# Pooled attention into a four-expert attention layer: score tiles of two heads and of 512 columns, split VectorE steps, a last batch in two parts, and a written-out order

## The chip, the cores and the metric

The kernel runs on one core of one Trainium2 chip. The metric is the device time of one execution in microseconds (us). The kernel before takes 198.42 us, the median of three runs (197.89, 198.42 and 199.59).

A core has five engines with instruction queues of their own: TensorE (PE) multiplies matrices, VectorE (DVE) and ScalarE (ACT) work element by element, GpSimd (POOL) does so too, and SyncE (SP) issues DMA transfers. Arithmetic results of PE go to PSUM, a small memory that DVE and ACT read; all other tiles lie in SBUF.

## The reference

The inputs are q, k and v (8 batches, 8 heads, 576 rows of 64), and the weights of four experts. Two attentions follow one another.

```python
# first attention: keys and values are means over 8 rows, so 72 of them
k_p = k.reshape(B, H, Sp, pool, D).mean(axis=3)
v_p = v.reshape(B, H, Sp, pool, D).mean(axis=3)
attn = softmax(q @ k_p.T / sqrt(64))
x = (attn @ v_p) as (8, 576, 512)

# second: a gate picks two of four experts for each row
logits = x @ w_gate
w = softmax over the two largest logits of a row, 0 for the others
for e in range(4):
    q, k, v = x @ wq[e], x @ wk[e], x @ wv[e]          # 576 x 64 each
    a = softmax(causal(q @ k.T / sqrt(64)))            # 576 x 576, lower triangle
    out += w[:, e] * (a @ v @ wo[e])                   # 576 x 512
```

The output is f32, 8 x 576 x 512. Every expert is computed for all rows, and the gate's weight is multiplied in at the normalisation.

## The kernel before, in words

**Tiles.** A row index of 576 is cut into five chunks: four of 128 and one of 64. Heads come in two halves of four; experts in two pairs (0, 1) and (2, 3), a pair filling 128 partitions with its two 64-wide projections. All matmul operands are bf16. Scores are computed transposed, keys on the partitions, so that exponentials can be used as the next product's operand as they are. A column of ones beside the values gives the softmax sum, and no maximum is subtracted. At the end a check looks at all reciprocals of the sums; if one lies outside a range, a branch runs a slow general version of all batches.

**Steps.** The program is planned as some hundred steps a batch, each named by two letters. For a batch:

- `ld`/`ln`: POOL issues the DMA loads of k, q and v in two halves each (line 324); the transfer turns f32 into bf16. `ln` marks the landing. The first batch's loads, the mask for the pooling product and the identity are issued in `first` (from line 780).
- `pk`, `pv`: the mean over 8 rows as a PE product with a mask `pm` (line 375); `kp`, `kz`, `kt`, `kT`: pooled keys copied, doubled, transposed on PE, copied. `vp`: pooled values copied.
- `qm`, `qc`: q transposed on PE and copied; for batches 5 to 7 by DMA instead (`qd` on SP, `ql` the landing).
- `am`, `ae`: pooled scores of one head on PE (line 437), and their exponential on ACT (line 462), for eight heads; and a ninth group with the one row in nine that a head's pairing leaves over (lines 450 and 472). `al`: POOL places the ninth group's results in the tile `eta` (line 483).
- `om`, `on`: output of the first attention for a chunk and half of the heads (line 493), then on DVE the reciprocal of the sum (505) and the product with it (506), into `xtm`.
- `xm`, `xc`: x transposed on PE and copied (batches 0 to 2), or `xd`, `xl`: turned by DMA (batches 3 to 7), into `xT`.
- `jm`, `jc`: the q and k projections of an expert pair and half of the rows, eight groups of four matmuls over 288 columns (line 550), and their copies. `vm`, `vc`: values of all experts and the gate's logits for a chunk (line 531), and the copies (541, 542).
- `ga`, `gs`, `ge`, `gb`, `gc`: the gate: maxima and selection on DVE (570 to 576), subtraction on POOL, exponential on ACT, weights on POOL, reciprocal and product on DVE.
- `bm`, `be`, `bk`: expert scores of a pair, in four parts of 400 columns for each of two experts (line 625), exponential on ACT (635), causal mask on POOL for each diagonal block (644).
- `bo`, `bn`: output of one expert for all five chunks, 15 matmuls (line 659); on DVE reciprocal (671), product with the gate's weight (673) and normalisation (674) into `osc`.
- `ot`, `oc`: `osc` transposed on PE and copied, or `od`, `ol`: turned by DMA (batches 2 to 6).
- `ym`, `yc`, `ys`: the product with wo for a chunk (line 695), the copy to SBUF (707), the store, issued on SP (712).
- At the end, `fl`, `fm`, `fc`: the range check on DVE, its sum on PE, the flag. The flag is then loaded into registers of all five engines (line 1319) and all five take the branch (1320).

**Turns.** A DMA transpose is issued on SP (line 778). All turns wait until the last input of the last batch has landed.

**Room.** Two PSUM tiles of two banks each, `jt`, serve the pooling products and both kinds of scores. Four one-bank PSUM tiles serve everything else. Inputs have three buffers for each of k, q and v; most work tiles have two, by the batch's parity.

**Order.** All instructions are emitted in one order, which sets the order in every engine's queue. It is found while the program is built, by the list scheduler `run_order` (line 169): it keeps a model time for each engine, takes the ready step with the lowest key (tables `RANK` and `EXTRA`, and the batch number times `SPAN`), and charges the durations of `COST`. Pooling products and both kinds of scores, and the dummy products between them, use 64 rows of the PE array, two matmuls side by side; all other products use 72 or 128 rows. The scheduler charges `TURN` for a change between the two kinds and prefers to stay in one. Where PE has nothing to do in the first 40 us of model time, it issues dummy products, four matmuls each (`filler`, line 745). Where a copy can go to ACT or DVE, the scheduler decides.

## Time and profile before

| | |
|---|---|
| profiled execution, device time | 198.56 us |
| its span, first to last instruction | 196.7 us |
| mean granted PE clock | 0.973 |
| input and weight bytes read from HBM | 30.42 MB |
| bytes written | 9.44 MB |
| loads of k, q, v, issue to landing (POOL's queue) | 10.2 to 10.3 us median |
| turns of x by DMA, issue to landing (SP's queue) | 2.5 us median |

The profile is of one execution. Its page lists each engine's busy time and share of the span, a picture of the span in 40 slices of 4.9 us (a digit is a tenth of the slice; the row PEclk is the clock that PE was granted, in tenths of full speed), the chain of work that ended last, followed back from the last instruction, and the costliest groups of instructions. PE overlaps its matmuls and its weight loads (PEld), and the ends of matmuls are modelled, so a busy share of PE is not PE at its best. The chain is a share of the span: what lies on it delays the end if it takes longer, and what does not may grow until it does.

### The profile page before, as it was taken

Reading aid. Unit: us, or ns where it says so; the run is one execution under the profiler, and the core shown is the slowest. Engines: PE = TensorE matmul, PEld = TensorE weight load, DVE = VectorE, ACT = ScalarE, POOL = GpSimd, SP = SyncE. Lnnn points to the kernel's source line nnn. Section 1 sums busy time; section 2 is a strip of 40 time slices with the busy share of each in tenths; the row PEclk is TensorE's granted clock in tenths of the full one; section 3 lists DMA queues with packets and bytes.
Section 4 is the critical chain, followed back from the end, with each engine's and each line's share of the span. In section 5 each row is a group of like instructions: output and inputs, shape, how many; then the busy total and the mean of one; then the engine's idle time right before and its main releaser. Section 6 shows DMA issues by size and latency. Waiting matters only on the chain.

```text
span 196.7 us, 6292 instructions
## 1 busy us (share of the span) xinstructions
PE 176.6 (90%) x2470; PEld 131.0 (67%) x2478; DVE 137.5 (70%) x478; ACT 139.7 (71%) x280; POOL 91.8 (47%) x197
## 2 busy tenths in 40 slices
PE   7999789899999899999789999889979999997740
PEld 7998668677889666766567658664657767575410
DVE  5122678938988787886934798769977868765840
ACT  3057588589994887866928896858979697788640
POOL 7957585765589553440405327314233533444100
PEclk9999999999999999999958999999999999999996
DMA  4999999999999999997955359362841559381561
GB/s 62 184 188 207 205 206 200 205 207 207 206 207 207 206 236 279 164 173 250 141 107 99 53 137 252 63 83 78 226 91 24 112 90 289 83 215 37 216 246 28
DMA packets 47666, 31.78 MB, mean 162 GB/s; under 512 B 28944, under 2 KB 43024, under 8 KB 47632
## 3 DMA queue, kind: packets, MB, share of 16 engines
q0 software_dynamic: 15056, 15.21, 47.3%
q1 hardware_dynamic: 32576, 16.13, 35.7%
q8 instruction: 20, 0.33, 0.7%
q14 instruction: 14, 0.11, 0.2%
HBM read 30.42 MB, written 9.44 MB: 203 GB/s over the span
## 4 chain that ended last, share of the span: by engine, by line
PE 65%; DMA 12%; DVE 9%; POOL 4%; ACT 4%; issue 2%; SPq 0%; POOLq 0%; ACTq 0%
PE p_ps L550 15%; PE v_ps L531 10%; PE y_ps L695 8%; PE jt L375 6%; PE jt L625 6%; DMA xT<-xtm 6%; DMA qb<-in_q_dram 6%; PE ob_ps L659 6%; PE oa_ps L493 4%; PE jt L437 4%; PE qt_ps L423 2%; DVE osc L674 2%; ACT etb L635 1%; PE xt_ps L518 1%; POOL kb L324 1%
## 5 line engine op out<-in xcount | busy, mean ns | idle before, releaser
L635 ACT ACTIVATE etb<-jt 128x800 bf16<-128x800 f32 x64 | 50.5, 845 | 8.8 <-PE jt L625 8.5
L644 POOL TENSOR_SCALAR_AFFINE_SELECT etb<-etb 128x256 bf16<-128x256 bf16 (+1 forms) x80 | 30.4, 389 | 53.6 <-ACT etb L635 52.5
L462 ACT ACTIVATE eta<-jt 72x512 bf16<-72x512 f32 x64 | 35.4, 595 | 6.3 <-PE jt L437 5.6
L506 DVE TENSOR_TENSOR xtm<-oa_ps,za 128x256 bf16<-128x256 f32 (+1 forms) x80 | 33.8, 423 | 2.7
L531 PE MATMUL v_ps<-wvg,xT 128*128 128x260 bf16 x160 | 24.5, 285 | 3.6 <-DMA xT<-xtm 3.5
L483 POOL COPY eta<-etl 72x256 bf16<-72x256 bf16 x16 | 20.0, 1456 | 9.6 <-ACT etl L472 9.6
L550 PE MATMUL p_ps<-xT,wk_sb 128*128 128x288 bf16 x128 | 20.7, 287 | 0.7 <-DVE wk_sb L830 0.7
L550 PE MATMUL p_ps<-xT,wq_sb 128*128 128x288 bf16 x128 | 20.8, 288 | 0.0
L695 PE MATMUL y_ps<-wo_sb,oT 128*128 128x512 bf16 x72 | 19.2, 380 | 1.6 <-ACT oT L689 0.8
L531 PEld LDWEIGHTS <-xT 128*128 128x128 bf16 x160 | 14.3, 100 | 9.1 <-DMA xT<-xtm 4.2
L625 PE MATMUL jt<-qTb,kTb 64*128 64x224 bf16 (+5 forms) x256 | 18.9, 253 | 1.4 <-ACT etb L635 1.1
L493 PE MATMUL oa_ps<-vpa,eta 72*128 72x65 bf16 x320 | 18.7, 194 | 0.6 <-DVE xtm L506 0.4
L659 PEld LDWEIGHTS <-etb 128*128 128x128 bf16 x480 | 17.1, 99 | 1.7 <-issue 0.6
L493 PEld LDWEIGHTS <-eta 72*128 72x128 bf16 x320 | 14.4, 98 | 5.7 <-issue 2.3
L659 PE MATMUL ob_ps<-vau,etb 128*128 128x65 bf16 x480 | 18.1, 196 | 0.0
L707 ACT COPY y<-y_ps 128x512 f32<-128x512 f32 (+1 forms) x26 | 14.8, 585 | 4.1 <-PE y_ps L695 2.9
L375 PEld LDWEIGHTS <-pm 64*72 64x72 bf16 x288 | 15.5, 110 | 1.9 <-issue 1.3
L505 DVE RECIPROCAL za<-oa_ps 128x4 f32<-128x4 f32 (+1 forms) x80 | 13.8, 172 | 4.2 <-PE oa_ps L493 4.0
L674 DVE TENSOR_TENSOR osc<-ob_ps,gt 128x320 bf16<-128x320 f32 x32 | 15.7, 491 | 1.1
L749 PE MATMUL p_ps<-warm 128*128 128x128 bf16 (+1 forms) x200 | 14.9, 236 | 1.2 <-DVE warm L781 1.2
L437 PE MATMUL jt<-qT,kpT 64*72 64x256 bf16 x128 | 15.7, 285 | 0.0
L749 PEld LDWEIGHTS <-warm 128*128 128x128 bf16 (+1 forms) x200 | 13.8, 106 | 1.4 <-DVE warm L781 1.2
(98 smaller groups left out, 286.9 us busy)
## 6 DMA issues: line engine op xcount, KB each, us to landing
out_dram<-y SPq DMA_DIRECT2D x32, 256.0 KB, 2.4
kb<-in_k_dram POOLq DMA_DIRECT2D x16, 288.0 KB, 10.3
qb<-in_q_dram POOLq DMA_DIRECT2D x16, 288.0 KB, 10.3
vb<-in_v_dram POOLq DMA_DIRECT2D x16, 288.0 KB, 10.2
out_dram<-y SPq DMA_DIRECT2D x8, 128.0 KB, 2.8
xT<-xtm SPq DMA_TRANSPOSE x25, 2.5
wqs<-in_moe_wq_dram POOLq DMA_DIRECT2D x1, 256.0 KB, 10.2
wo_sb<-in_moe_wo_dram POOLq DMA_DIRECT2D x1, 256.0 KB, 10.7
```

Source lines behind the costliest of these rows:

```text
L375: nc.tensor.matmul(out=jt[0:SK, hh, 0 : HQ * D], lhsT=pm[r, t, :], rhs=kv[r, t], start=(t == 0), stop=(t == TG - 1),)
L462: nc.scalar.activation(out=eta[i][:, n, 0:S] .rearrange("p (g t) -> p g t", t=TG)[:, :, t0 : t0 + 8] .rearrange("p g (i w) -> p g i w", w= ...
L493: nc.tensor.matmul(out=oa_ps[:, h, :], lhsT=eta[i][:, 4 * w + h, c * 128 : (c + 1) * 128], rhs=vpa[iv][:, 4 * w + h, :], start=True, stop= ...
L506: nc.vector.tensor_tensor(out=xtm[i][0:n, c, :].rearrange("p (f h e) -> p h f e", f=NF, h=H)[:, 4 * w : 4 * w + 4], in0=oa_ps[0:n, :, 0:D] ...
L531: nc.tensor.matmul(out=v_ps[:], lhsT=xT[i][:, f, c * 128 : (c + 1) * 128], rhs=wvg[:, f, :], start=(f == 0), stop=(f == NF - 1),)
L550: nc.tensor.matmul(out=p_ps[:], lhsT=w_sb[:, f, g, :], rhs=xT[i][:, f, w * HALF : (w + 1) * HALF], start=(f == 0), stop=(f == NF - 1),)
L625: nc.tensor.matmul(out=jt[:, ee, o : o + z - a], lhsT=kTb[i][r, g, kc * 128 : (kc + 1) * 128], rhs=qTb[i][r, g, a:z], start=True, stop=True,)
L635: nc.scalar.activation(out=etb[i][g][:, :, 400 * part : 400 * (part + 1)], in_=jt[:, :, 0:400], func=EXP, scale=B_SCALE,)
L644: nc.gpsimd.affine_select(out=et[:, :, o : o + w], in_=et[:, :, o : o + w], pattern=[[0, 2], [1, w]], compare_op=ISGE, fill=0.0, base=0, c ...
L659: nc.tensor.matmul(out=ob_ps[:, c, :], lhsT=etb[i][e // 2][:, e % 2, o : o + 128], rhs=vau[iv][:, kc, e, :], start=(kc == 0), stop=(kc == c),)
L695: nc.tensor.matmul(out=y_ps[:], lhsT=oTs[g][:, c, :], rhs=wo_sb[:, g, :], start=(g == 0), stop=(g == NP - 1),)
L749: nc.tensor.matmul(out=p_ps[:, j * 128 : (j + 1) * 128], lhsT=warm[0:r], rhs=warm[0:r], start=True, stop=True,)
```

## The change

**Two heads at once.** The pooled scores of two heads go into one `jt` tile, so a batch has five `am`/`ae` groups in place of nine. Each pair is still followed by two exponentials of 512 elements. Their write pattern into `eta` is turned: one pass over the nine-row groups is now innermost, so that neighbouring elements in the instruction lie nine apart in the tile, and its read takes one bank after the other instead of alternating.

**Expert tiles of 512 columns.** A pair's scores go in three parts of 512 columns, and the last 64 columns of both pairs share a seventh part, in place of four parts of 400 for each pair. One tile `etb` holds both pairs. Masks: nine a batch in place of ten, the one of the last block for both pairs at once.

**Split steps.** The reciprocal of the first attention is a step of its own (`oi`), so is that of the second (`bi`), the product with the gate's weight (`bg`, into a constant tile), and the gate's maxima come in four steps, its reciprocal in one more. Between them the order can put other DVE work.

**Last batch in two parts.** Batch 7's expert outputs, norms, transposes and their copies are done for chunks 0 to 2 and then for chunks 3 and 4. Its last two stores are issued on ACT. The range check looks at all earlier batches ahead (`fo`) and at the last one's alone behind (`fn`).

**Branch without GpSimd.** The flag is loaded by PE, ACT, DVE and SP, and only these take the branch; the general version uses no POOL instruction any more, and its loop over batches is written out eight times. Its causal mask is a constant, made at batch 6's gate.

**Start.** POOL issues the first half of batch 0's q ahead of the two instructions that make the mask `pm`. Batch 1's halves come in the order k, q, (gate weights), k, q, v, v in place of k, q, v, k, q, v, (gate weights).

**Order.** `run_order` and its tables are gone. A string `ORDER` lists all steps, with a letter for the engine of a copy (`a` ACT, `d` DVE) and `f` or `F` for a dummy product of 128 or 64 rows, now two matmuls long; there are 77 of them (50 of four before). Among the copies, ACT has three of q, four of x, two of pooled values and five of expert values fewer, and five of projections more.

```diff
+ORDER = """
+lh0.1 lh0.2 lh0.0 lh0.3 lh0.4 lh0.5 f f f f f f f f f f f f f f f f f f ln0.0 f f f f f f f f f
+f f f f ln0.1 pk0.0 ld1.0 F F ld1.2 kp0.0a F F ln0.2 F F F F wi0.3 kz0.0 F F F kt0.0 ln1.0 ld1.1
...
+bk1.1 on4.3 xd3.0 ql5.0 bm1.4 vp7.0d jm2.6 be1.4 bo1.1 jc2.6d qd6.0 xl3.0 bo1.0 bi1.1 bk1.5
+bg1.1 am5.2 bi1.0 bn1.1 am5.4 ae5.2 bo1.3 bg1.0 bn1.0 bo1.2 bi1.3 ae5.4 bg1.3 ot1.0 bi1.2 bn1.3
+am5.3 xd3.3 ql6.0 vm3.0 bg1.2 oc1.0a bn1.2 jm2.5 vc3.0d ae5.3 ot1.1 xd3.2 jc2.5d ym0.2 oc1.1d
...
+ot7.3 fl7.0 oc7.3d fm7.0 ys7.1 yc7.2a yd6.4 ym7.3 fc7.0 ym7.4 ys7.2 yc7.3a yd7.0 yc7.4d yt7.0
+yd7.1 yt7.1 yd7.2 yd7.3 yd7.4 fv7.0
+"""
+def emit(steps, filler):
+    place = {}
+    for st in steps:
+        place.setdefault(st.name[0] + str(st.name[1]), []).append(st)
+    for word in ORDER.split():
+        if word in ("f", "F"):
+            filler(word == "F")
+            continue
+        e = {"a": "ACT", "d": "DVE"}.get(word[-1])
+        at, n = (word[:-1] if e else word).split(".")
+        st = place[at][int(n)]
+        assert not st.done and all(d.done for d in st.deps)
+        st.done = True
+        st.fn(e)
...
     SPLIT = [
-        [(0, 0, 400, 0)],
-        [(0, 400, 576, 0), (1, 128, 352, 176)],
-        [(1, 352, 576, 0), (2, 256, 432, 224)],
-        [(2, 432, 576, 0), (3, 384, 576, 144), (4, 512, 576, 336)],
+        [(0, 0, 512, 0)],
+        [(0, 512, 576, 0), (1, 128, 576, 64)],
+        [(2, 256, 576, 0), (3, 384, 576, 320)],
     ]
...
-        if n < H:
-            t0 = (n % HQ) % 2
-            nc.scalar.activation(
-                out=eta[i][:, n, 0:S]
-                .rearrange("p (g t) -> p g t", t=TG)[:, :, t0 : t0 + 8]
-                .rearrange("p g (i w) -> p g i w", w=2),
-                in_=jt[0:SK, 0:2, 0 : 4 * NG].rearrange("p w (i g) -> p g i w", g=NG),
+        if n < len(PAIRS):
+            for z, h in enumerate(PAIRS[n]):
+                t0 = (h % HQ) % 2
+                nc.scalar.activation(
+                    out=eta[i][:, h, 0:S]
+                    .rearrange("p (g t) -> p g t", t=TG)[:, :, t0 : t0 + 8]
+                    .rearrange("p g (i w) -> p w i g", w=2),
+                    in_=jt[0:SK, :, z * 4 * NG : (z + 1) * 4 * NG].rearrange(
+                        "p w (i g) -> p w i g", g=NG
+                    ),
...
+    def ob_inv(b, e, cs, ob_ps):
+        nc.vector.reciprocal(
+            out=zb[:, b, cs[0] : cs[-1] + 1, e : e + 1], in_=ob_ps[:, :, HD : HD + 1]
+        )
+
+    def ob_gate(b, e, cs, G):
+        c0, c1 = cs[0], cs[-1] + 1
+        nc.vector.tensor_mul(
+            out=gzb[:, b % 2, c0:c1, e : e + 1], in0=zb[:, b, c0:c1, e : e + 1], in1=G[:, c0:c1, e : e + 1]
+        )
...
-    def y_store(c, dst, y):
+    def y_store(c, dst, y, eng):
         n = 128 if c < NC - 1 else 64
-        nc.sync.dma_start(out=dst, in_=y[0:n])
+        eng.dma_start(out=dst, in_=y[0:n])
...
         T["in", 0, "k"] = load_in("k", srcs["k"][0])
+        T["in", 0, "q"] = new_in("q")
+        load_half(T["in", 0, "q"], srcs["q"][0], 0)
         for lo in range(2):
             nc.gpsimd.affine_select(
...
-        T["in", 0, "q"] = load_in("q", srcs["q"][0])
+        nc.scalar.copy(out=pm[NG:], in_=pm[0:NG])
+        load_half(T["in", 0, "q"], srcs["q"][0], 1)
...
+        halves = (range(NC),) if b < B - 1 else (range(3), range(3, NC))
...
+        add(
+            ("fv", last),
+            lambda: nc.values_load(T["fc", last][0:1, 0:1], engines=GENERAL, min_val=0, max_val=768),
+            [("fc", last)],
+        )
...
     with tc.If(bad > 0, label="general"):
-        with tc.For_i(0, B, 1) as gb:
+        for gb in range(B):
             general_batch(gb)
```

765 lines of the change are left out of this document (362 added, 403 removed), and 52 rows, old and new, of tables (EXTRA, RANK).

## The prediction

> **What bounds the kernel now.** The page comes first: the span, each engine's busy time, the clock row, and who ended the chain.
>
> ```profile
> span 196.7 us, 6292 instructions
> PE 176.6 (90%) x2470; PEld 131.0 (67%) x2478; DVE 137.5 (70%) x478; ACT 139.7 (71%) x280; POOL 91.8 (47%) x197
> ...
> PEclk9999999999999999999958999999999999999996
> ...
> PE 65%; DMA 12%; DVE 9%; POOL 4%; ACT 4%; issue 2%; SPq 0%; POOLq 0%; ACTq 0%
> ```
>
> TensorE (PE) is busy for 176.6 of 196.7 us, and the chain that ended last runs over PE for 65% of the span. Of the rest, 12% is DMA, 9% VectorE (DVE). Every other engine is below 72%. PE's granted clock is full except near slice 20. The profiled execution took 198.56 us, 1.86 us outside its span; the median of the three timed runs is 198.42, so a sum made against 198.56 stands 0.14 us too high, which I neglect.
>
> A busy share does not say how dense the work is, so next come windows of 8 us (columns: length, busy time of PE, its weight loads, DVE, ScalarE (ACT), GpSimd (POOL), clock, DMA share, GB/s), a good stretch first, then the poor ones.
>
> ```profile
> 48.00:56.00 8.00, 8.00 (x133) 6.33 (x130) 7.39 (x32) 7.65 (x14) 5.26 (x12) 1.00 1.21 206
> 96.00:104.00 8.00, 6.18 (x70) 4.40 (x67) 4.11 (x16) 4.11 (x9) 1.89 (x6) 0.59 0.60 86
> 136.00:144.00 8.00, 6.73 (x72) 3.60 (x71) 7.31 (x30) 7.62 (x16) 3.20 (x9) 1.00 0.71 183
> 190.00:196.70 6.70, 0.00 (x0) 0.00 (x0) 0.00 (x0) 0.00 (x0) 0.00 (x0) 0.73 0.35 127
> ```
>
> In 48 to 56 us PE has no idle time. In 96 to 104 it idles 1.82 us and its clock is at 0.59. In 136 to 144 it idles 1.27 us while ACT works 7.62 of 8 us. The last 6.7 us hold no arithmetic at all. So four things can be won: time between pieces of work on a busy PE, the hole near 97 us, the waits on ACT and DVE in the middle, and both ends. I take the parts of the change in that order.
>
> **Fewer switches between two kinds of matmul.** Pooling, both score products and half of the dummy products use 64 rows of the array; all else uses 72 or 128 rows, in one tile. The timeline shows what a switch costs (columns: start, duration of the merged group, engine, line, operation).
>
> ```profile
> 172.09 0.66 PE L550 MATMUL p_ps<-xT,wk_sb 128*128 128x288 bf16 x4
> 172.59 0.65 PE L550 MATMUL p_ps<-xT,wq_sb 128*128 128x288 bf16 x4
> 173.08 0.65 PE L550 MATMUL p_ps<-xT,wk_sb 128*128 128x288 bf16 x4
> 173.67 0.56 PE L625 MATMUL jt<-qTb,kTb 64*128 64x144 bf16 x8
> ...
> 174.66 0.65 PE L550 MATMUL p_ps<-xT,wk_sb 128*128 128x288 bf16 x4
> 175.25 0.35 PE L625 MATMUL jt<-qTb,kTb 64*128 64x176 bf16 x4
> ```
>
> Four projections follow four projections 0.50 and 0.49 us after their start. Where expert scores follow, it is 0.59 us, twice (173.08 to 173.67, 174.66 to 175.25). So a switch costs 0.10 us. In program order the old kernel has 162 switches, 147 of them behind its last dummy product; the new one has 124 and 109. Two causes: pooled scores are issued for two heads at once (five groups in a batch in place of nine), and expert scores come in seven groups in place of eight. 38 switches x 0.10 = 3.8 us. PE is in the chain for 65% of 196.7 = 128 us, about 0.8 of the 160 us between 24 and 184, so I take 3.0 (0 to 3.8). Streamed columns don't change: 1600 for each expert before and after. The 64 matmuls fewer I cost at nothing, since columns set their time.
>
> **The hole near 97 us.**
>
> ```profile
> 94.59 4.39 DMA xT<-xtm
> 99.02 1.05 PE L531 MATMUL v_ps<-wvg,xT 128*128 128x260 bf16 x4 [1.69 <-DMA xT<-xtm]
> ...
> 105.21 0.61 PE L531 MATMUL v_ps<-wvg,xT 128*128 128x260 bf16 x4
> ```
> ```profile
> 153.54 0.92 PE ob_ps L659 x30
> ```
>
> Batch 3 is the first whose x is turned by DMA. The value product at 99.02 waited 1.69 us for it, and the four matmuls of such a product take 1.05 us there and 0.61 at 105.21. A clock of 0.59 over 8 us loses 3.3 us, 0.9 of it inside idle time; so the hole costs 1.8 idle + 2.4 slow = 4.2 us. In the new order ten PE steps stand between the first turn of batch 3 (xd3.0) and the value product that needs it (vm3.0): four expert outputs (two of them, x30, take 0.92 at the full clock), one projection group of 0.49, one group of five transposes, and four small score groups. That is 1.8 + 0.5, for the other five some 1.3 (up to 0.28 each, half of the eight score matmuls of 173.67), and six switches of 0.10: 4.2 us, about the 4.39 that the turn took. I expect most of the wait to go and take 2.8 of 4.2 (ends: 4.2 gone; or the stall moves to the turn behind it, xd3.3, which now stands behind the query turn qd6.0 on SP, with a second dip like this one, -4.2).
>
> [...]
>
> **DVE steps split, copies shared out anew.** Reciprocal, gate product and normalisation are now steps of their own, and so are four parts of the gate.
>
> ```profile
> 104.79 0.17 DVE L572 TENSOR_TENSOR mx<-hi 128x5 f32<-128x5 f32 x1
> 104.87 0.16 DVE L573 TENSOR_TENSOR mn<-hi 128x5 f32<-128x5 f32 x1
> 104.94 0.16 DVE L574 TENSOR_TENSOR ml<-lo 128x5 f32<-128x5 f32 x1
> 105.14 0.17 DVE L575 TENSOR_TENSOR mn<-mn,ml 128x5 f32<-128x5 f32 x1
> ```
>
> Three independent small instructions start 0.07 to 0.08 us apart, the one that needs the third 0.20 later. An independent instruction put between a reciprocal and its user can save 0.12 us of DVE. There are 112 such pairs (80 + 32), so up to 13 us of a DVE that is busy 70%. That is not the bound; it shortens what PE waits for only where DVE or ACT is late, as in 136 to 144. By number, ACT hands DVE three copies of qT, four of xT, two of vpa and five value copies, and takes five projection copies, so DVE gets a little busier and ACT a little less. I take 1.0 us from all this. Ends: +5, if half of the roughly 10 us of PE idle time and ACT/DVE links of the chain between 24 and 184 goes; -4, if DVE, with the added copies, becomes the late one.
>
> **Score tiles of two heads and of 512 columns on ACT.**
>
> ```profile
> L635 ACT ACTIVATE etb<-jt 128x800 bf16<-128x800 f32 x64 | 50.5, 845 | 8.8 <-PE jt L625 8.5
> ...
> L462 ACT ACTIVATE eta<-jt 72x512 bf16<-72x512 f32 x64 | 35.4, 595 | 6.3 <-PE jt L437 5.6
> ...
> L707 ACT COPY y<-y_ps 128x512 f32<-128x512 f32 (+1 forms) x26 | 14.8, 585 | 4.1 <-PE y_ps L695 2.9
> ```
> ```profile
> 13.81 2.81 ACT L462 ACTIVATE eta<-jt 72x512 bf16<-72x512 f32 x5
> ```
> ```profile
> L483 POOL COPY eta<-etl x16: 1312/1439/1862, 14.0 to 136.2; 72x256 bf16<-72x256 bf16 x16
> ```
> ```profile
> L644 POOL TENSOR_SCALAR_AFFINE_SELECT etb<-etb 128x256 bf16<-128x256 bf16 (+1 forms) x80 | 30.4, 389 | 53.6 <-ACT etb L635 52.5
> ```
>
> 800 elements take 845 ns and 512 take 595: 0.87 ns an element. 48 exponentials of 1024 (1037 ns) and 8 of 256 (373) make 52.8 us in place of 64 x 845 = 54.1. The pooled exponentials keep their number and size, but the write pattern turns: it was eight elements side by side, and is now every ninth. No ACT row of this trace writes so. Lower end: nothing, and no gain either, since today's exponential (595) costs what a plain copy of 512 costs (585). Upper end: POOL writes the same tile in steps of nine elements, and its 256 elements take 1312 ns at least where a mask over 256 takes 389, so 3.6 ns an element, or 1.85 us an exponential. I take nothing: the nearer rows are ACT's own, and its read, which alternates between two banks, is free.
>
> [...]
>
> **The start.**
>
> ```profile
> 1.41 1.49 POOL L324 DMA_DIRECT2D kb<-in_k_dram  x2 [0.89 <-POOLq L1337]
> 2.98 1.65 POOL L785 TENSOR_SCALAR_AFFINE_SELECT pm<-pm 64x648 bf16<-64x648 bf16 x2
> 4.58 1.23 POOL L324 DMA_DIRECT2D qb<-in_q_dram  x2
> ```
> ```profile
> 9.94 11.81 DMA qb<-in_q_dram
> ```
>
> The chain waits until 21.79 us for the second half of batch 1's q, issued at 9.94 behind the queue's earlier loads. The first half of batch 0's q now goes ahead of the two mask instructions (1.65 us), and batch 1's v no longer stands before that second half: nine halves stand before it, not ten. Eleven halves have landed by 21.75, the first two issued from 1.41 on, so one takes at most 20.3 / 11 = 1.85 us; I take 1.5, since the first starts late. So q comes about 1.5 us earlier; PE has about 0.5 us less done by then (pooled outputs come later). I take 1.0 (0 to 2.3).
>
> **The end.**
>
> ```profile
> 187.36 1.90 PE y_ps L695 x8
> ...
> 189.33 0.58 ACT y L707
> ```
> ```profile
> 181.58 0.84 ACT L635 ACTIVATE etb<-jt 128x800 bf16<-128x800 f32 x1 [0.34 <-PE jt L625]
> ...
> 182.92 7.74 SPq L712 DMA_DIRECT2D out_dram<-y  x10
> ```
> ```profile
> L1319 SPq TENSOR_LOAD <-flag x1: 1177/1177/1177, 190.7 to 190.7; - x1
> ...
> L1348 POOLq EVENT_SEMAPHORE  x4: 17/17/17, 195.9 to 196.6; - x4
> L1348 POOLq DRAIN  x3: 40/103/4406, 191.4 to 196.4; - x3
> L1348 SPq DRAIN  x3: 7/7/13, 194.3 to 196.1; - x3
> ```
>
> The last copy ends at 189.91, the span at 196.7: 6.8 us. SP issues its last store until 190.67, then loads the flag and is ready at 194.3. But POOL, which loads the flag too, starts a drain of 4.4 us at 191.4 and reaches the barrier only at 195.9; from there 0.8 us are left. Without its branch POOL drains right behind its last mask, in the shade of the last outputs. That is worth 195.9 - 194.3 = 1.6 us. ACT now issues the last two stores, and the flag is ready before the last copies, so SP can load it earlier: 0.4 more, 2.0 in all (0 if the drain itself waits for the end; 2.5 at most).
>
> Ahead of that, the last exponential ends at 182.42 (181.58 + 0.84), 7.5 us before the last copy. With the last batch in two parts only the first part of two experts stands behind it: mask 0.5, six matmuls 0.4, two norms of three fifths the size 1.2, transposes and copy 0.9, ten output matmuls 2.3 (eight took 1.90), a gap of 0.7 for the second transpose and its copy, copy 0.6: 6.6. I take 0.9 (0 to 1.5; the added small instructions are in it).
>
> **Sum.** 3.0 + 2.8 + 1.0 + 0 + 1.0 + 2.0 + 0.9 = 10.7; 198.56 - 10.7 = 187.9 us.
>
> **The rivals.** *A, DVE and ACT waits fall too:* the middle gives 5 in place of 1, and the hole closes whole: 187.9 - 4 - 1.4 - 1 = 181.5. For it: in 136 to 144 DVE (7.31) and ACT (7.62) are both nearly full. Against: the two together keep their 137.5 and 139.7 us of work. *B, the gain is given back:* only the end (2.9) and the start hold, each switch saved becomes a wait for an exponential: a tile of two heads is freed after two exponentials (2 x 595 ns). 198.56 - 3.9 = 194.7. Against: two such tiles exist, as before. *C, the list changes nothing that counts:* a dip elsewhere eats the gain of the end, 198. *D, slower:* the write in steps of nine makes ACT the bound. ACT's best window is 7.65 of 8, so 13.8 to 182.4 us have room for 161 us, and 139.7 are used: 22 us, 0.34 us for each of 64 exponentials, is where it begins to decide. At a third of POOL's surcharge, 0.62 us, it is 40 us, 18 over: 187.9 + 18 = 206. Against: no ACT row shows a price for a pattern.
>
> **How the numbers follow.** Forecast (183 to 193): 0.56. A 0.14, B 0.12, C 0.07, D 0.11. The likeliest gives 188. From 179.5 (A, less 2) to 196.5 (B, plus 2) lie the forecast, A and B, 0.82. Runs of this kernel lie 0.3% below and 0.6% above their median, so 1% is about what can be told from no change. Forecast, A and B are faster by over 1% (below 196.4): 0.82; C within: 0.07; D slower: 0.11.
>
> **What would show it.** Right: pooled exponentials still near 595 ns; the clock row without a slice below 9 between 20 and 180 us; POOL's long drain begun before the last copy, and under 5.2 us from the last copy to the span's end; PE's last matmul near 178 to 180 us. Wrong: exponentials over 0.9 us, a DMA turn or a DVE norm with a PE wait of over 1 us behind it, or a second dip of the clock.

## The result and the profile after

The changed kernel takes 302.87 us (median of 4 runs, 302.52 to 304.57), the kernel before 198.34. The ratio is 1.527, interval 1.518 to 1.536. In this document medians are of all runs, and ratios leave out the runs that took over 1.5% longer than the fastest of the same kernel. The prediction said 188.0, 179.5 to 196.5: it was wrong by more than 100 us. Its slow rival D had the mechanism, at a third of the price.

The page of the changed kernel, in the order in which the one before was read (span, busy times, the slices of ACT and the clock, the chain):

```profile
span 301.5 us, 6043 instructions
PE 209.9 (70%) x2356; PEld 149.2 (49%) x2368; DVE 135.8 (45%) x507; ACT 243.7 (81%) x258; POOL 89.8 (30%) x190
...
ACT  2296999869985877679978999999898987468971
...
PEclk9966555597768977875559659589978879999997
...
ACT 46%; PE 35%; issue 7%; DMA 5%; DVE 4%; POOL 1%; SPq 0%; ACTq 0%; DVEq 0%
ACT eta L359 42%; PE jt L272 6%; PE p_ps L455 5%; DMA xT<-xtm 5%; PE v_ps L436 4%; PE ob_ps L587 3%; PE p_ps L689 3%; PE oa_ps L392 3%; PE jt L549 3%; PE y_ps L631 3%; PE jt L334 2%; PE qt_ps L320 2%; DMA oT<-osc 1%; DVE y L643 1%; ACT etl L371 1%
```

ACT has gone from 139.7 to 243.7 us busy and from 4% of the chain to 46%, nearly all of it one line, 359. The clock row, full before but for one place and the end, is now low in more than half of its slices, and PE is busy for 33 us more with fewer instructions.

The groups behind it (busy time, mean ns of one, idle time before and what ended it):

```profile
L359 ACT ACTIVATE eta<-jt 72x512 bf16<-72x512 f32 x64 | 148.6, 2630 | 10.6 <-PE jt L334 10.6
L565 ACT ACTIVATE etb<-jt 128x1024 bf16<-128x1024 f32 (+1 forms) x56 | 50.8, 954 | 10.4 <-PE jt L549 10.0
...
L392 PE MATMUL oa_ps<-vpa,eta 72*128 72x65 bf16 x320 | 25.3, 217 | 19.1 <-ACT eta L359 18.6
...
L334 PE MATMUL jt<-qT,kpT 64*72 64x256 bf16 x128 | 16.0, 341 | 22.1 <-ACT eta L359 21.9
```

The 64 pooled exponentials take 2630 ns each in place of 595. Neighbours overlap by some 0.3 us, so their busy time, 148.6 in place of 35.4 us, is what ACT lost: 113.2 us, 1.77 each. The expert exponentials are near where the prediction had them (56 x 954 ns = 53.4 us; forecast 52.8, or 52.9 by its own 0.87 ns an element). PE waits for line 359 wherever it needs its result (18.6) or a free score tile (21.9).

### The profile page after: what moved, and what is told of

Same layout as the page of the kernel before. It is cut to its first block, busy times and chain, and to the rows that moved or that the text cites. A ratio compares the mean times of both kernels' runs of the same rounds, so it can differ in the third digit from the quotient of the medians.

```text
span 301.5 us, 6043 instructions
## 1 busy us (share of the span) xinstructions
PE 209.9 (70%) x2356; PEld 149.2 (49%) x2368; DVE 135.8 (45%) x507; ACT 243.7 (81%) x258; POOL 89.8 (30%) x190
## 4 chain that ended last, share of the span: by engine, by line
ACT 46%; PE 35%; issue 7%; DMA 5%; DVE 4%; POOL 1%; SPq 0%; ACTq 0%; DVEq 0%
ACT eta L359 42%; PE jt L272 6%; PE p_ps L455 5%; DMA xT<-xtm 5%; PE v_ps L436 4%; PE ob_ps L587 3%; PE p_ps L689 3%; PE oa_ps L392 3%; PE jt L549 3%; PE y_ps L631 3%; PE jt L334 2%; PE qt_ps L320 2%; DMA oT<-osc 1%; DVE y L643 1%; ACT etl L371 1%
## 5 line engine op out<-in xcount | busy, mean ns | idle before, releaser
L359 ACT ACTIVATE eta<-jt 72x512 bf16<-72x512 f32 x64 | 148.6, 2630 | 10.6 <-PE jt L334 10.6
L565 ACT ACTIVATE etb<-jt 128x1024 bf16<-128x1024 f32 (+1 forms) x56 | 50.8, 954 | 10.4 <-PE jt L549 10.0
L572 POOL TENSOR_SCALAR_AFFINE_SELECT etb<-etb 128x256 bf16<-128x256 bf16 x72 | 29.2, 419 | 79.7 <-ACT etb L565 72.9
L392 PE MATMUL oa_ps<-vpa,eta 72*128 72x65 bf16 x320 | 25.3, 217 | 19.1 <-ACT eta L359 18.6
L334 PE MATMUL jt<-qT,kpT 64*72 64x256 bf16 x128 | 16.0, 341 | 22.1 <-ACT eta L359 21.9
L436 PE MATMUL v_ps<-wvg,xT 128*128 128x260 bf16 x160 | 28.6, 318 | 2.9 <-DMA xT<-xtm 2.9
L272 PEld LDWEIGHTS <-pm 64*72 64x72 bf16 x288 | 22.0, 149 | 17.1 <-issue 15.2
L549 PE MATMUL jt<-qTb,kTb 64*128 64x64 bf16 (+4 forms) x192 | 19.8, 304 | 7.0 <-ACT eta L359 6.3
L272 PE MATMUL jt<-vb,pm 64*72 64x256 bf16 x144 | 14.6, 369 | 10.0 <-ACT eta L359 9.9
L334 PEld LDWEIGHTS <-kpT 64*72 64x72 bf16 x128 | 7.8, 129 | 25.4 <-issue 23.9
L455 PEld LDWEIGHTS <-wq_sb 128*128 128x128 bf16 x128 | 12.5, 107 | 8.1 <-issue 4.1
```

Of the source, the lines that this page charges most:

```text
L272: nc.tensor.matmul(out=jt[0:SK, hh, 0 : HQ * D], lhsT=pm[r, t, :], rhs=kv[r, t], start=(t == 0), stop=(t == TG - 1),)
L334: nc.tensor.matmul(out=jt[0:SK, w, z * 4 * NG : (z + 1) * 4 * NG], lhsT=kpT[w * D : (w + 1) * D, h, :], rhs=qT[w * D : (w + 1) * D, p0 : p ...
L359: nc.scalar.activation(out=eta[i][:, h, 0:S] .rearrange("p (g t) -> p g t", t=TG)[:, :, t0 : t0 + 8] .rearrange("p g (i w) -> p w i g", w= ...
L392: nc.tensor.matmul(out=oa_ps[:, h, :], lhsT=eta[i][:, 4 * w + h, c * 128 : (c + 1) * 128], rhs=vpa[iv][:, 4 * w + h, :], start=True, stop= ...
L436: nc.tensor.matmul(out=v_ps[:], lhsT=xT[i][:, f, c * 128 : (c + 1) * 128], rhs=wvg[:, f, :], start=(f == 0), stop=(f == NF - 1),)
L455: nc.tensor.matmul(out=p_ps[:], lhsT=w_sb[:, f, g, :], rhs=xT[i][:, f, w * HALF : (w + 1) * HALF], start=(f == 0), stop=(f == NF - 1),)
```

## The experiments

### The write pattern, alone and undone

Theory W: the new write order of the pooled exponentials made the whole loss. Rival O: the written-out order or the tiles of two heads carry a part of it. Two runs separate them: the changed kernel with the old write, and the kernel before with the new one. Both edits turn the read along with the write; the run of single patterns further down tells these two apart.

```diff
-                    .rearrange("p g (i w) -> p w i g", w=2),
+                    .rearrange("p g (i w) -> p g i w", w=2),
                     in_=jt[0:SK, :, z * 4 * NG : (z + 1) * 4 * NG].rearrange(
-                        "p w (i g) -> p w i g", g=NG
+                        "p w (i g) -> p g i w", g=NG
```

> The changed kernel with the write of the pooled exponentials back to eight elements side by side (and the read that goes with it). Theory W, the write pattern alone made the loss: the 64 exponentials fall from 2630 ns to 570 to 650, ACT from 243.7 us busy to about 114, the clock returns to over 0.95, and the time is what the other terms of the forecast give, 183 to 193 us. Rival O, the written-out order or the tiles of two heads carry a part of the loss of their own: the exponentials are as short, but the time stays over 200 us, and PE waits of several us remain that no exponential ends.

```diff
-                .rearrange("p g (i w) -> p g i w", w=2),
-                in_=jt[0:SK, 0:2, 0 : 4 * NG].rearrange("p w (i g) -> p g i w", g=NG),
+                .rearrange("p g (i w) -> p w i g", w=2),
+                in_=jt[0:SK, 0:2, 0 : 4 * NG].rearrange("p w (i g) -> p w i g", g=NG),
```

> The kernel before with only the new write (and read) pattern of the pooled exponentials; still one head to a tile, the old order. Theory W: each exponential takes 2.4 to 2.8 us, ACT is busy for 139.7 + 64 x 2.03 = 270 us, and the time is 285 to 325 us. Rival O, the price comes only with two heads in a tile: exponentials under 1 us and a time within 198 to 215.

The same kernel as the first of these was run a second time, beside two that follow below:

> The changed kernel with the old write once more, so that the two next to it are compared with it in the same call: 190.5 to 193, 0.96 to 0.975 of the kernel before.

The old write in the changed kernel: 191.83 us, ratio 0.967 (0.957 to 0.976), and the second time 190.90, ratio 0.964 (0.957 to 0.970).

The new write in the kernel before: 303.61 us, ratio 1.530 (1.516 to 1.545), the time of the changed kernel. Lines of both pages, the changed kernel with the old write first:

```profile
span 188.8 us, 6043 instructions
PE 169.4 (90%) x2356; PEld 127.3 (67%) x2368; DVE 132.9 (70%) x507; ACT 132.5 (70%) x258; POOL 90.0 (48%) x190
...
PEclk9999699999999999999999999999999999999995
...
L359 ACT ACTIVATE eta<-jt 72x512 bf16<-72x512 f32 x64 | 33.8, 593 | 10.7 <-PE jt L334 10.7
```

```profile
span 300.0 us, 6292 instructions
PE 217.7 (73%) x2470; PEld 156.2 (52%) x2478; DVE 140.0 (47%) x478; ACT 249.3 (83%) x280; POOL 92.0 (31%) x197
...
L462 ACT ACTIVATE eta<-jt 72x512 bf16<-72x512 f32 x64 | 150.1, 2599 | 3.7 <-PE jt L437 3.3
```

Theory W holds on both sides: the one line makes 302.87 us out of 191, and about 304 out of 198. (My 114 us for ACT with the old write was too low; it is 132.5. I had taken off 64 times the difference of the durations, which overlap.) Everything else in the change is together a gain of 3 to 4%.

### What a write pattern costs

The third pattern, two elements side by side and then a step of nine, in the changed kernel (`"p g (i w) -> p i g w"` on the write, `"p w (i g) -> p i g w"` on the read):

> The changed kernel with a third pattern: two elements side by side, then a step of nine elements. If the price is for each run that begins in another place (theory of runs), there are 256 runs in place of 512 and the exponential takes about 595 + 1.0 = 1.6 us, ACT about 180 us busy, the time 205 to 245 us. If the price is for each element, or for the order of the loops, it stays at 2.4 to 2.8 us and about 300 us.

```profile
L359 ACT ACTIVATE eta<-jt 72x512 bf16<-72x512 f32 x64 | 64.9, 1157 | 8.0 <-PE jt L334 7.7
```

209.53 us, ratio 1.056 (1.047 to 1.065). By busy time an exponential costs 1.01 us, against 0.53 with eight side by side and 2.32 with one: in these three patterns, all of 512 elements, the price goes with the number of separate places (64, 256 and 512), not with the elements. It is less than in proportion (0.48 for 256 runs, 1.79 for 512). I had expected 1.6 us.

This run shows one thing more. ACT is busy for 160.0 us, 27.5 more than with the old write, and the kernel takes some 18 us longer, though ACT had been idle for 56 us of the span. By the prediction's room of 161 us, below which ACT's work was to cost nothing, there should have been no loss.

Then the price by itself, without the computation:

```python
for nm, step in (("a_s1", 1), ("a_s2", 2), ("a_s3", 3), ("a_s4", 4), ("a_s8", 8), ("a_s9", 9), ("a_s16", 16)):
    dst = stepped(nm, step)                     # 72 x 512 bf16, one element every `step`
    for _ in range(REP):                        # 6
        nc.scalar.activation(out=dst, in_=plain(one), func=EXP)
# ... runs of 2, 4, 8 in steps of 9; the changed kernel's own pattern; f32 in steps of 1, 4, 9;
# a copy in steps of 9; a read in steps of 9; then the same on DVE and POOL
```

> Leaves the whole computation out and writes zeros; it only times instructions over 72 x 512 elements with different write patterns, six of each back to back, on ACT, then DVE, then POOL. Theory of runs that begin over 16 bytes apart: on ACT steps of 1 to 4 elements of bf16 (2 to 8 bytes) near 0.6 us, a step of 8 (16 bytes), 9 and 16 near 2.6 us, runs of 2, 4 and 8 in steps of 9 near 1.6, 1.1 and 0.85 or less, f32 in steps of 4 and 9 as slow as bf16 in steps of 8; a copy as slow as an exponential. Rival, any element that isn't beside the last one pays: a step of 2 is at 2.6 us already. Rival, the price lies in the read or in the four loops: a step of 9 alone is near 0.6 us. POOL with steps of 9 near 2.6 us for 512 (1.3 for 256 in the kernel); DVE isn't known, and would be near 2.6 us if the price is the memory's and not the engine's.

Windows of this run, one for six instructions (columns: window, its length, busy time of ACT with a number that takes in neighbours at the edges, clock, DMA share, GB/s). In order, on ACT: steps of 1, 2, 4, 8 and 9 elements of bf16, runs of 2 and of 8 in steps of 9, the changed kernel's pattern, f32 in steps of 4:

```profile
4.68:8.30 3.62, 3.46 (x6) 1.00 1.01 328
8.30:12.73 4.43, 4.27 (x8) 1.00 1.02 363
...
18.77:26.48 7.71, 7.55 (x7) 1.00 0.95 337
26.48:40.81 14.33, 14.17 (x8) 1.00 0.39 137
40.81:55.19 14.38, 14.22 (x7) 1.00 0.00 0
...
69.01:75.85 6.84, 6.68 (x7) 1.00 0.00 0
...
80.28:83.90 3.62, 3.46 (x8) 1.00 0.00 0
83.90:98.01 14.11, 13.95 (x8) 1.00 0.00 0
...
101.95:108.27 6.32, 6.16 (x7) 1.00 0.00 0
```

Then DVE in steps of 1 and 9, and POOL in steps of 1 and 9 (busy times of DVE, ACT and POOL):

```profile
136.67:139.30 2.63, 2.45 (x6) 0.00 (x0) 0.00 (x0) 1.00 0.00 0
...
149.61:157.32 7.71, 7.54 (x8) 0.00 (x0) 0.00 (x0) 1.00 0.00 0
...
160.91:164.83 3.92, 0.00 (x0) 0.00 (x0) 3.61 (x6) 1.00 0.00 0
...
179.40:194.45 15.05, 0.00 (x0) 0.00 (x0) 14.73 (x7) 1.00 0.00 0
```

One instruction is a sixth of a window: on ACT 0.60 us side by side, 0.74 in steps of 4 bytes, 1.29 of 8, 2.39 of 16, 2.40 of 18, and (not shown) 1.01 of 6 and 2.30 of 32. So among the steps timed it grows up to 16 bytes, from 4 on by 0.14 us a byte (1.65 us for 12 bytes), and is about the same at 18 and 32. The expectation had no price below 16 bytes and one jump there; that was an assumption of mine, and the run shows a slope.

Eight side by side in steps of nine cost nothing (0.60), which is what the kernel before wrote. The changed kernel's pattern costs 2.35, the same as a plain step of nine, so neither the order of its loops nor its read adds anything; a copy costs as much as an exponential (2.34). f32 in steps of 16 bytes takes 1.05, where the expectation had it as slow as bf16. DVE goes from 0.44 to 1.29, half of ACT's price, and POOL from 0.65 to 2.51, so the price is not the memory's alone. Both rivals written down fall: at 4 bytes the price is 0.14 us and not the whole, and the read is not what costs, though a bf16 read from SBUF in steps of nine took 1.14, against 0.60 for the plain f32 read from PSUM (a plain bf16 read from SBUF was not timed).

### The start: too few dummy products

With the old write one low place is left in the clock row, in slice 5. The timeline of PE in this kernel (start, duration of the group, engine, line, operation, wait):

```profile
16.29 0.27 PE L272 MATMUL jt<-kb,pm 64*72 64x256 bf16 x1
19.03 1.14 PE L272 MATMUL jt<-kb,pm 64*72 64x256 bf16 x17 [2.47 <-DMA kb<-in_k_dram]
19.93 1.86 PE L272 MATMUL jt<-vb,pm 64*72 64x256 bf16 x18
...
22.16 1.93 PE L320 MATMUL qt_ps<-ident,qb 128*128 128x128 bf16 x18
```

PE waits 2.47 us for batch 1's keys and then does its transposes in 1.93 us, which took 1.18 before. The clock is at half from 20.35 to 23.76 us. 18 dummy products more, put ahead of that wait:

```diff
-F F ae0.2 F pk1.0 ln0.4 ln0.5 ln1.4 pv0.0 ld1.5 kp1.0d ld2.0 kz1.0 am0.1 vp0.0d qm1.0 ld2.2
+F F ae0.2 F
+F F F F F F F F F F F F F F F F F F
+pk1.0 ln0.4 ln0.5 ln1.4 pv0.0 ld1.5 kp1.0d ld2.0 kz1.0 am0.1 vp0.0d qm1.0 ld2.2
```

> The changed kernel with the old write of the exponentials (191.83 us), and 18 more dummy products of 64 rows ahead of batch 1's key pooling, where PE waited 2.47 us for the load and its clock then fell to half for 3.4 us. Theory K, the idle time took the clock: no low clock between 0 and 180 us, the transposes of q behind it take 1.2 us in place of 1.93, and the time falls by 1.0 to 2.0 us, to 189.8 to 190.8. Rival, the start is bound by the loads anyway (the chain names them at 9.2 and 30.6 us): the clock stays up, but later waits eat it, and the time stays within 0.5 us of 191.8.

190.10 us, ratio 0.960 (0.954 to 0.966): 0.8 to 1.7 us below the two sets of runs without it, whose intervals overlap with it. The profile shows what the time alone doesn't settle, the page's clock row first, then PE's timeline:

```profile
PEclk9999999999999999999999999999999999999997
```
```profile
14.94 2.84 PE L691 MATMUL p_ps<-warm 64*128 64x128 bf16 x48
17.62 0.27 PE L274 MATMUL jt<-kb,pm 64*72 64x256 bf16 x1
18.38 1.14 PE L274 MATMUL jt<-kb,pm 64*72 64x256 bf16 x17 [0.49 <-DMA kb<-in_k_dram]
...
20.65 1.18 PE L322 MATMUL qt_ps<-ident,qb 128*128 128x128 bf16 x18
```

The low stretch is gone, the transposes take 1.18 again, and from 8% of the work on this kernel stays about 2 us ahead of the same one without the dummies (table below). The changed kernel aside, six traces with this start and without the added dummies all have a low clock for 3.4 or 6.8 us that begins between 17 and 21 us; the two traces with them (this one and `turns_early` below) have none. So the dummies keep the clock up. That the idle time took it, as theory K had it, isn't shown by this: the dummies take away idle time and add work at once. The section on the hole returns to that.

### The end: two parts, stores, POOL

Three parts of the change are taken back, each alone, in the changed kernel with the old write. The last batch in one part:

```diff
-        halves = (range(NC),) if b < B - 1 else (range(3), range(3, NC))
+        halves = (range(NC),)
```

> The changed kernel with the old write, and the last batch's expert outputs, norms, transposes and copies in one part again (in the order string the words of the second part go, and those of the first stand where the later of the two stood). The forecast put the two parts at 0.9 us (0 to 1.5): from the last expert exponential to the last copy 0.9 us more than with two parts. Rival, the two parts cost as much as they save (their added small steps, PE with nothing else to do): within 0.3 us of it, or less.

194.63 us, ratio 0.975 (0.967 to 0.982), an interval that overlaps with those of the old write. From the last expert exponential to the last copy the trace has 9.5 us in place of 7.4, the clock full in both, so two parts are worth 2.1 us in this order by these two traces. In the other traces with two parts the stretch is 7.5 to 8.3 us, so 1.2 to 2.1 in all, more than the 0.9 forecast; in the kernel before, whose order was made for one part, the same stretch took 7.5.

All stores on SP:

```diff
     def late(b, c):
-        return b == B - 1 and c >= NC - 2
+        return False
...
-ym7.4 ys7.2 yc7.3a yd7.0 yc7.4d yt7.0 yd7.1 yt7.1 ...
+ym7.4 ys7.2 yc7.3a yd7.0 yc7.4d ys7.3 yd7.1 ys7.4 ...
```

> The changed kernel with the old write, all stores on SP again. With two stores on ACT, 5.8 us lie between the last copy and the end of the span, and ACT's own issues (2.74 us for two) end last. If ACT's issues are what is late, the stretch shortens to 5.0 to 5.4 us; if SP's queue is (its earlier stores end at 182.2), it grows to 6.0 to 6.8 us.

192.44 us, ratio 0.964 (0.957 to 0.971), no difference in the time. The stretch from the last copy to the end of the span is 6.1 in place of 5.9 us: of the two expectations the second, at its edge. But other traces that end as the changed kernel does have 5.0 to 5.8 us there, so one trace of each can't settle 0.2.

POOL in the flag load and the branch again:

```diff
-GENERAL = [getattr(mybir.EngineType, e) for e in ("PE", "Activation", "DVE", "SP")]
+GENERAL = [getattr(mybir.EngineType, e) for e in ("PE", "Activation", "DVE", "Pool", "SP")]
```

> The changed kernel with the old write, the flag loaded by all five engines and all five taking the branch. The forecast put POOL's 4.4 us drain behind the branch at 1.6 us of the end: the stretch from the last copy to the end of the span grows from 5.8 to 6.8 to 7.5 us, and POOL's long drain starts behind the flag. Rival, the drain waits for something else that lies at the end whatever POOL does (not for POOL's own place in its queue): the stretch stays at 5.8 us.

190.55 us, ratio 0.962 (0.955 to 0.969): no loss. The instructions of the end, by line (number, ns least/median/most, first and last start), without POOL and then with it:

```profile
L1278 SPq EVENT_SEMAPHORE  x8: 17/17/17, 183.6 to 187.2; - x8
...
L1306 POOLq DRAIN  x3: 40/108/4860, 175.6 to 188.6; - x3
L1306 SPq DRAIN  x3: 7/7/13, 188.0 to 188.3; - x3
```
```profile
L1278 SPq EVENT_SEMAPHORE  x8: 17/17/17, 184.6 to 188.0; - x8
...
L1306 POOLq DRAIN  x3: 40/103/4406, 183.6 to 189.5; - x3
L1306 SPq DRAIN  x3: 7/7/13, 188.8 to 189.2; - x3
```

POOL's drain does move, from 175.6 (right behind its last mask) to 183.6, as forecast. But it then ends at 188.0, and SP isn't through its waits behind the branch before 188.0 either. What SP waits for there is the landing of the stores: in the trace with POOL the last one lands at 187.87 and the wait for it ends at 187.90, in the trace without at 187.02 and 187.06. So the rival's number holds, but not its reason: the drain moves with POOL's place in the program, and what lies at the end whatever POOL does is the last store. The stretch is 5.9 us without POOL and 5.7 with it.

### The middle: the turns' waits

How far the changed kernel with the old write is ahead of the kernel before can be followed through the work. I counted, in each trace, the streamed columns of all matmuls but dummies (half for those of 64 rows, which run two side by side: in the first timeline of the start, 17 of 256 columns take 0.90 us from start to start, 4.8 columns a ns, where four of 288 with 128 rows in the prediction take 0.50, 2.3), and looked when a given share of the total was reached:

```
share of the work   before   old write   ahead   with warm start   ahead
  4%                  21.1        22.8    -1.6        21.0         +0.1
  8%                  30.0        31.0    -1.0        28.8         +1.2
 16%                  42.3        43.4    -1.1        41.2         +1.2
 32%                  67.9        67.4    +0.5        65.2         +2.7
 48%                  94.1        93.5    +0.6        91.4         +2.7
 52%                 105.4        99.2    +6.2        97.4         +8.1
 64%                 126.3       120.7    +5.6       118.0         +8.3
 80%                 155.2       147.8    +7.5       144.5        +10.7
 84%                 161.5       156.2    +5.3       153.0         +8.6
100%                 189.2       181.9    +7.3       180.2         +9.0
```

Each column is one trace; four other traces of the old write without added dummies are 1.8 to 3.2 us behind at 4%. The largest step, 5.6 us, lies between 48 and 52%: the hole near 97 us. Between 80 and 84% some 2.1 us are given back, and the windows show where, in the kernel with the old write (columns as in the prediction):

```profile
96.00:104.00 8.00, 8.00 (x80) 5.26 (x78) 6.15 (x19) 6.91 (x15) 2.82 (x4) 1.00 1.05 231
104.00:112.00 8.00, 6.39 (x106) 4.22 (x103) 6.04 (x30) 6.77 (x13) 4.41 (x14) 1.00 0.66 93
...
144.00:152.00 8.00, 6.83 (x75) 5.15 (x75) 4.60 (x16) 4.05 (x10) 0.87 (x3) 1.00 0.80 170
152.00:160.00 8.00, 6.57 (x76) 4.37 (x76) 4.12 (x21) 5.76 (x12) 2.94 (x10) 1.00 0.69 160
```

96 to 104 is full now. In 104 to 112 and 144 to 160 PE idles 1.2 to 1.6 us in each window, each time in one wait of 1.1 to 1.6 us for a turn of x. The chain of this kernel has the turns that end these waits (start, issue to landing):

```profile
106.49 4.65 DMA xT<-xtm
...
146.83 3.94 DMA xT<-xtm
...
152.34 3.59 DMA xT<-xtm
```

The median of the 25 turns of x in this trace is 2.5 us; each of these three takes 1.1 to 2.1 us more, about as long as PE waits. On top of the warm start, three turns (xd6.1, xd7.4, xd7.2) stand further ahead in SP's queue, and so does the projection for which batch 7's turns wait:

```diff
-xd6.2 xl6.4 bn4.1 ym3.0 yc3.3d be5.4 ym3.4 bk4.5 ys3.1 ...
+xd6.2 xd6.1 xl6.4 bn4.1 ym3.0 yc3.3d be5.4 ym3.4 bk4.5 ys3.1 ...
...
-bm4.3 jc5.4a on7.1 ...
+bm4.3 jc5.4a jm5.7 jc5.7a on7.1 ...
...
-jc6.2d xl6.1 jm5.7 jc6.3d ym3.2 ys3.0 jc5.7a ol4.1 jm6.6 xd7.4 yc3.2a ...
+jc6.2d xl6.1 jc6.3d ym3.2 ol4.1 jm6.6 xd7.4 ys3.0 yc3.2a ...
```

> The changed kernel with the old write and the 18 dummy products (190.10 us), and in the order string four words moved ahead on SP: the turn xd6.1 right behind xd6.2, xd7.4 and xd7.2 ahead of a store each, and the projection jm5.7, for which batch 7's turns wait, some forty words earlier. If the waits of 1.1 to 1.4 us between 136 and 156 us come from the place of the turns in SP's queue, one or two of the three go and the time falls by 1 to 2 us, to 188 to 189. Rival, PE's own order makes up for each wait elsewhere, or the turns wait for DVE: within 0.5 us of 190.1.

190.03 us, ratio 0.956 (0.950 to 0.963), beside 190.10: the rival holds. In the trace this kernel is as far ahead at 80 and at 84% of the work as the one without the edit (10.7 and 8.3 us). The edit aimed at more than it could win: the trace with the warm start alone has two waits of over 1 us for a turn of x left, at 107.9 and 151.4 us. With the turns moved ahead there are still two in the same places, and each ends with a turn that took 4.3 and 3.4 us. So it is less the place of these turns in SP's queue than their own length. Why some turns take up to twice the median stays open.

### The hole near 97 us

The prediction counted the low clock there together with a wait of 1.69 us. The turn that PE waited for had taken 4.39 us, against a median of 2.5, as those of the section before. But windows of 1 us of the kernel before show the clock going down in the same moment as the wait begins, not behind it:

```profile
96.00:97.00 1.00, 0.87 (x16) 0.57 (x13) 0.93 (x5) 1.00 (x3) 0.41 (x2) 1.00 1.94 143
97.00:98.00 1.00, 0.33 (x4) 0.10 (x3) 0.93 (x5) 1.00 (x2) 0.92 (x3) 0.74 0.05 5
98.00:99.00 1.00, 0.00 (x0) 0.00 (x0) 0.64 (x3) 0.39 (x1) 0.54 (x2) 0.50 0.54 100
```

A mean of 0.74 over 97 to 98 puts the fall at 97.49, 0.16 us behind PE's last matmul. Dummy products in the wait itself were to tell:

```diff
+    def v_warm(b, i, c):
+        if b == 3 and not warmed:
+            warmed.append(c)
+            for _ in range(7):
+                filler(None)
+        return v_mm(i, c)
```

> The kernel before with 28 dummy matmuls of 128 rows (some 1.8 us) ahead of batch 3's first value product, that is inside the wait near 97 us. If the wait took the clock, as the prediction had it, the low clock of 6.8 us goes and the time falls by 2.4 us or a little more. If the clock is set in steps of 3.41 us by the work of the step before (it fell at 97.49, 0.2 us behind the start of the wait, and the stretch ahead of it had little work in it), a low step near 97 us stays, alone, and the time falls by 1.0 to 1.9 us, half as much.

197.91 us, ratio 1.000 (0.996 to 1.004). The edit missed its place: the first value product of batch 3 is not the one that waits, but one at 90 us (its chunk had been turned at 83), so the 1.9 us of dummies stand 7 us ahead of the hole. They delay the work, the wait shrinks from 1.69 to 0.63 us, and no low clock is left in the trace; the time is the same. It tells nothing of the two theories. What the low clock near 97 us is worth can only be estimated: the kernel before was timed 28 times in the two sets of runs to which this one and the warm start belong, and the three executions with a granted clock of 0.995, which leaves no room for such a stretch, took 196.4 to 196.6 us, some 1 to 2 us under the medians (197.5 and 198.47). The prediction had 2.4.

The traces themselves tell the two theories apart. In all of them a low clock lasts a whole multiple of 3.41 us (3.41, 6.83, 10.24 and so on), but for the one that the end cuts off. I cut every trace of a whole kernel so far into these stretches (715 in twelve traces) and summed in each the streamed columns, every matmul weighted by its rows over 128. A dense stretch holds 8192: in the run of PE alone, below, 80 matmuls of 512 columns and 128 rows start in 17.00 us, so 16 in 3.41. Whether the next stretch is granted the full clock is told by this sum in 712 of 715 cases, with the limit at 3100 (38%), chosen on these same traces; the best limit on idle time misses 43. Stretches with 1.6 to 1.8 us of idle time and a sum over 3100 were followed by the full clock, one with 0.11 us and a sum of 2880 by half. One of the three misses is the stretch ahead of the fall at the start, with a sum of 3200 and 2.10 us of idle time. The stretch ahead of the fall at 97.49 has 0.51 us of idle time, but a sum of 2950: first-attention outputs of 72 rows and scores of 64.

A last run tested this, without the computation: PE alone, with matmuls of 512 columns in stages.

```python
dense(128, 100); dense(64, 100); dense(128, 50); dense(32, 100); dense(128, 50)
gaps(4, 12)      # rounds of four with 128 rows, a copy on ACT between them
dense(128, 50)
gaps(2, 16)      # rounds of two
dense(128, 50)
```

> Leaves the whole computation out and writes zeros; PE runs stages of matmuls over 512 columns: dense with 128 rows, dense with 64, with 128, with 32, with 128, then rounds of four matmuls with a copy on ACT between the rounds, dense, rounds of two, dense. Theory of work: the granted clock is set for 3.41 us by the streamed columns of the 3.41 us before, each weighted with its rows over 128, and falls under some 3100 of 8192 cycles (38%). Then 128 and 64 rows run at the full clock, 32 rows (25%) at half although PE is never idle, rounds of four (about 0.85 us of matmuls in 1.75, 49%) at the full clock with half of the time idle, rounds of two (about 33%) at half. Theory of idle time: every dense stage runs at the full clock, 32 rows too, and the rounds of four and of two have the same clock, or fall with their idle share, 51% and 67%.

Windows inside four of the stages, dense with 64 rows, dense with 32, rounds of four, rounds of two:

```profile
27.00:47.00 20.00, 20.00 (x94) 8.74 (x93) 0.00 (x0) 0.00 (x0) 0.00 (x0) 1.00 0.14 50
...
62.00:98.00 36.00, 36.00 (x85) 12.20 (x83) 0.00 (x0) 0.00 (x0) 0.00 (x0) 0.50 0.00 0
...
115.00:130.00 15.00, 8.64 (x35) 3.17 (x33) 0.00 (x0) 5.12 (x9) 0.00 (x0) 1.00 0.00 0
...
147.00:166.00 19.00, 11.12 (x22) 2.77 (x22) 0.00 (x0) 6.31 (x12) 0.00 (x0) 0.50 0.00 0
```

Dense matmuls of 32 rows, without a moment of idle time, run at half the clock for the whole stage; rounds of four run at the full one with PE idle for 42% of the window, and rounds of two at half with 41%. The theory of work holds on all four stages; that of idle time fails on the dense 32 rows. The rounds alone would not decide: in the first 3.41 us of the rounds of two, while the clock was still full, PE idled for 1.91 us, in the rounds of four for 1.37, so a limit between these two would fit them too. The stages put the limit of work between 25 and 50%; the 38% comes from the twelve traces.

## Why the prediction was wrong, step by step

**Score tiles of two heads, 0 us: the step that failed.** The prediction said: "I take nothing: the nearer rows are ACT's own, and its read, which alternates between two banks, is free." ACT's rows were near by engine, but none of them writes single elements in steps. The row that did, POOL's placement into the same tile in the same steps of nine, gave 1.85 us an exponential as the upper end; the trace has 1.77. So the upper end was the price, within 5%. That it was so near is luck: in the run of patterns POOL pays 1.86 us for steps of nine and ACT 1.80, but DVE 0.85. The prediction named that end and then left it out of its range: 118 us of ACT with 22 us of room is a time near 285, and the range stopped at 196.5 and gave the slow case 0.11.

**Rival D** named the mechanism and its place. It took a third of POOL's price, for no reason in a row, and so got 206. With the measured price its own sum is 98.7 us of other ACT work (132.5 - 33.8) + 148.6 = 247, 86 more than the 161 of room, on 188: 274. The other 29 us are the room itself. D took ACT to be busy for up to 7.65 of 8 us, 96%, from the first pooled exponential to the last expert one; in the changed kernel it is busy for 86% of that stretch and idle for 38.6 us, 35.9 of them in waits for PE. With the old write it is idle there for 37.0 us, in the kernel before for 37.5. So the 111 us more of ACT's work made the kernel 113 us longer, and none of it went into idle time. The pairs of elements (30.3 us idle) and the new write in the kernel before (30.6) used some 7 us of it. PE waits for ACT and ACT for PE, and PE, whose work has become thin, runs at a lower clock (a mean of 0.783, against 0.979 with the old write) and takes 209.9 us in place of 169.4 for the same products. How much of ACT's idle time is due to that clock wasn't tried.

**Fewer switches, 3.0, and DVE steps and copies, 1.0:** near the right size together. Outside the start, the hole and the end, the changed kernel with the old write gains 2.2 us between 4 and 48% of the work (0.6 of them by 8%, still at the start) and 1.1 behind 52%, so 3.3 at most in place of 4.0. A switch costs the same in both kernels (median 0.10 us, from start to start less the time of the columns), and there are 38 fewer. The two terms were not measured apart.

**The hole, 2.8 of 4.2:** 5.6, so the size was half of it, and more than the 4.2 that the hole was reckoned to cost: the new order's work there is dense (4% of the work in 5.7 us, 6.6 on the mean of that kernel). The reasoning was wrong in two places. The turn at 94.59 is not batch 3's first but its third (SP had issued two at 83.35). And by the sums over the stretches the clock did not fall for the wait but behind thin work (2950 columns of 8192, with 0.51 us of idle time). The end of -4.2, a second dip behind the next turn, did not come; the waits that did come, of 1.1 to 1.6 us, took 2 us back at 80 to 84% without a fall of the clock.

**The start, +1.0:** -1.6 at 4% of the work. Batch 1's second half of q, of which the prediction spoke, landed 1.3 us earlier (20.46 for 21.75, reckoned 1.5), and its keys let PE go 1.46 us earlier (19.03 for 20.49). The 0.5 us for less work at hand was the wrong size: PE had nothing for 2.47 us, and its clock fell behind that. With 18 more dummies the edit gives +1.2 at 8 and 16%, the term as forecast.

**The end, 2.0:** 0.9 (6.75 to 5.88 us from the last copy to the end of the span; 5.0 to 5.9 in six traces). POOL's drain, 1.6 of it, did end last in the kernel before (195.8, SP 194.3), but in the new order its absence buys nothing: with POOL back in the branch it ends together with SP's waits. Nor could SP be ready 0.4 earlier, since it waits for the last store, which lands 4.1 us behind the last copy for 3.4 before. **Two parts, 0.9:** 2.1 by taking them back, but only 0.1 against the stretch of before.

**The sum without the exponentials:** forecast 187.9 for a profiled run, 190.57 measured, a gain of 8.0 in place of 10.7; by the medians 190.9 and 191.8. Of the signs that the prediction set for being wrong the first, "exponentials over 0.9 us", came, and brought the other two with it (waits of up to 1.5 us for a turn, and a low clock in 26 of the 40 slices). With the old write only the waits for turns came, and a low clock at the start.

The experiments leave a better kernel than both: the changed one with the old write and 18 more dummy products, 190.1 us, 4% under the kernel before. That the dummies are worth some 2 us is read from the traces; the intervals of the times with and without them overlap.

## What to carry to other kernels

Price an access pattern by a row that has the same pattern, even on another engine, before one of the same engine without it, and then time it alone, since engines differ (for steps of nine DVE paid 0.85 us here, ACT 1.80). ACT's write of 512 bf16 elements in steps of 16, 18 and 32 bytes took 2.39, 2.40 and 2.30 us, four times the plain one (0.60), and the same reordering on the read side of PSUM was free here (593 to 595 ns with the read that alternates between banks). An engine's idle time need not be room: ACT's 37 us, nearly all of it waits for PE, took up at most 7 us of added work here. Where the two ends of an unknown price lie on both sides of an engine's room, the far end is a case with a time, and belongs in the range. Before giving PE's low clock to a wait, sum the work in the 3.41 us ahead of its fall.

## What was not expected of the hardware

In the twelve traces of whole kernels the granted clock of a 3.41 us stretch went with the work of the stretch before, counted with the rows in use: behind a sum under 3100 of 8192 columns (38%, a limit chosen on these traces) it was half, behind the others full, in 712 of 715 cases. Dense matmuls of 32 rows ran at half the clock for a whole window (0.50 over 36 us with PE 100% busy), and 1.6 us of idle time in a stretch did no harm where the rest of it was dense (a sum of 3694, in the kernel with the old write near 109 us). A busy share alone does not tell it: PE was busy for 58% of the window of the rounds of four, at the full clock, and for 59% of that of the rounds of two, at half. The traces show this agreement; what brings it about they do not show.

ACT's time for 512 bf16 elements in steps of 16 bytes, 2.39 us, is over twice its time for f32 in such steps (1.05), and its time in steps of 18 bytes, 2.40, nearly twice DVE's (1.29). Why bf16 costs more than f32 wasn't tried.
